# Clustered attention feeding a mixture of experts: expert scores as pairs of 64-row products, ten probability tiles, fixed banks and a new order

## The chip, the cores and the metric

The kernel runs on one core of one Trainium2 chip. A core has five engines that the text names: TensorE (PE; its weight loads are listed apart as PEld), VectorE (DVE), ScalarE (ACT), GpSimd (POOL) and SyncE (SP), which here only issues DMAs. The metric is device time in microseconds; the time of a kernel is the median of its runs.

## What is computed

```python
# clustered attention: batch 4, heads 8, sequence 768, head dim 64, 16 clusters per head
q_assign = argmax(einsum('bhsd,hcd->bhsc', normalized(q), normalized(centroids)))
k_assign = argmax(einsum('bhsd,hcd->bhsc', normalized(k), normalized(centroids)))
mask     = q_assign[:, :, :, None] == k_assign[:, :, None, :]
scores   = where(mask, q @ k.T / 8, -1e9)
attn_out = softmax(scores) @ v                         # per head
x        = attn_out as [batch, sequence, 512]
# mixture of experts: 4 experts of dim 64, causal attention in each, top 2 per token
logits = x @ w_gate
w      = softmax over the top 2 of logits
for e in range(4):
    qe, ke, ve = x @ wq[e], x @ wk[e], x @ wv[e]
    a   = softmax(where(causal, -1e9, qe @ ke.T / 8))
    out += (e is in the token's top 2) * w[e] * (a @ ve @ wo[e])
```

## The kernel before

The work is cut into 24 *pairs* n. The first 16 are pairs of attention heads (`attention_operands`), the last 8 pairs of experts (`moe_operands`), two to a batch; `core(n)` is common to both. The two heads (or experts) of a pair lie in rows 0 to 63 and 64 to 127 of the operand tiles.

*The order.* Every step is recorded as an operation of a `Plan`. A table of numbers, `ORDER`, then says in which order all operations are issued; each engine takes its own in that order, so an instruction that waits holds up all behind it on its engine. "~20" in the table stands for 20 fill matmuls (`spin`, L1150), which compute nothing that is used; "*" picks an operation's second engine. A second table, `SLOTS`, picks the buffer. PSUM has three double banks (`pp`, for scores, row scores and projections) and two single banks (`sg0`, `sg1`); which single bank a step gets is picked by `SLOTS`. The fills write sg0.

*An attention pair.* Per pair: k and q are turned by VectorE (L485, 128x768 with a strided writing side; pair 0 by TensorE, L494). The cluster of each row is found by a product with the centroids into a single bank (L520), which VectorE transposes into the other one (L524); a maximum, a comparison, a multiplication, a maximum and a one-hot comparison follow there (L531, L532, L533, L538, L539), then a transpose back (L527). ScalarE makes `rows` of it (L544), which go through DRAM (`rw`) into 16 rows of the operand tile `tk`. k and q themselves are each split into a rounded part (hi, ScalarE L333) and the rest (lo).

Row products (L887; two times two matmuls into one double bank: the hi parts, then 48 rows with the clusters) give a coarse score with queries on the partitions; VectorE takes its maxima (L900), gathers them (L906), turns them (L914), and a DMA puts them into a row of `tk`. The scores proper (L970) have keys on the partitions: per tile four steps (kh·ql, kh·qh, kl·qh, and 49 rows with clusters and maxima), each for both heads: the two matmuls of a step use rows 0 to 63 and 64 to 127 and run at the same time. ScalarE takes the exponential (L983) into a probability tile, GpSimd and VectorE add the tiles up (L338, L339), TensorE sums over keys (L1049, fp32, column tiles of 32) and multiplies with v (L1022, fp32, column tiles of 64; two recorded passes each). The results, normalised (L1099), go to DRAM as x, and from there to the expert part.

*An expert pair.* Projections of k and q for both experts together (L644, 12 full-height products into `pp` for each half of each), split by ScalarE and VectorE (L333, L653) into a staging tile `hl`. From there 10 DMAs a pair and two copies (L344, L345) put the parts of each expert one above the other, so that each of the two experts has full-height operands. The row products (L890, 80 rows) and the scores (L976: one step of 128 rows and one of 97) are full-height matmuls, one expert after the other. The causal triangle is added to the coarse scores by VectorE (L898). Their maxima are turned by TensorE (L928 into a single bank), negated by ScalarE or VectorE (L934, L937) and sent by DMA into a row of `tq`. GpSimd cuts the triangle out of the probabilities (L989). Values are projected at L694; the output product is L1137.

*Buffers.* Operand tiles `tk`, `tq` exist three times; attention uses them by n % 3, the experts two of them. Probability tiles are three of their own (p0 to p2) and, in turn, tiles lent by x (xh0 to xl2) or, for the experts, pieces of the third operand set.

## Time and profile before

| | before |
|---|---|
| median of three runs | 731.78 us (728.76, 731.78, 733.81) |
| profiled execution | 730.91 us, its span 729.2 us |
| TensorE busy | 683.1 us (94%) |
| VectorE busy | 496.7 us (68%) |
| GpSimd busy | 470.1 us (64%) |
| ScalarE busy | 294.4 us (40%) |
| mean granted TensorE clock | 0.979 |

The share of busy time is a mean over three stretches: the start up to about 55 us, the attention pairs to about 400 us, and the experts. Each has its own limit, so the rows below are taken by stretch. A busy TensorE is one that has matmuls in flight; what one of them costs is read from the distance of two starts.

### The profile page before, as it was taken

The page shows a single profiled execution, that of the slowest core. Times are in us where ns is not written, and L with a number is a line of the kernel's source. Part 1 is how long each engine was busy: PE and PEld are TensorE (multiplying, and loading weights), DVE is VectorE, ACT ScalarE, POOL GpSimd, SP SyncE. Part 2 cuts the span into 40 slices and gives each one's busy share as a digit, 9 for nine tenths or more (in the row PEclk, how much of TensorE's full clock was granted, in tenths as well). Part 3 has the DMA queues.
Part 4 walks back from the last instruction along what each step waited for, and adds up shares of the span by engine and source line. Part 5 has one row for each costly group of instructions (what it writes and reads, how often), then busy time and mean ns, then how long its engine had stood idle before and what let it go on. Part 6 is the DMA issues. An engine that isn't in the chain of part 4 may idle for free. (4 is left out here: it accounts for less than half of the span.)

```text
span 729.2 us, 13595 instructions
## 1 busy us (share of the span) xinstructions
PE 683.1 (94%) x5230; PEld 509.5 (70%) x5230; DVE 496.7 (68%) x808; ACT 294.4 (40%) x500; POOL 470.1 (64%) x344
## 2 busy tenths in 40 slices
PE   5589999999999999999999999989989799999997
PEld 4566667676767676766666777669668776797775
DVE  3577888697689889889787442554564376657843
ACT  2314464545554544454445153324141414242441
POOL 3227799999999987999995675761535433331420
PEclk9699999999999999999999999999899999999999
DMA  7134444165272445344142441433243435334423
GB/s 131 43 77 80 102 99 78 47 141 106 67 176 55 110 99 126 79 104 110 45 142 79 117 132 36 144 104 88 88 110 89 110 95 140 102 82 125 118 83 115
DMA packets 140729, 72.52 MB, mean 99 GB/s; under 512 B 116700, under 2 KB 125176, under 8 KB 140664
## 3 DMA queue, kind: packets, MB, share of 16 engines
q1 hardware_dynamic: 140664, 71.65, 39.4%
q8 instruction: 41, 0.67, 0.4%
q14 instruction: 24, 0.20, 0.1%
HBM read 39.68 MB, written 16.06 MB: 76 GB/s over the span
## 5 line engine op out<-in xcount | busy, mean ns | idle before, releaser
L900 DVE TENSOR_REDUCE mx<-pp 128x2 f32<-128x768 f32 (+1 forms) x224 | 206.0, 940 | 75.0 <-PE pp L887 65.6
L970 PE MATMUL pp<-tq,tk 64*128 64x384 f32 x1152 | 137.4, 343 | 1.4 <-DVE mx L900 0.7
L970 PEld LDWEIGHTS pp<-tq,tk 64*128 64x128 f32 x1152 | 98.9, 185 | 15.6 <-DVE mx L900 2.9
L983 ACT ACTIVATE p<-pp 128x768 f32<-128x768 f32 (+2 forms) x99 | 76.1, 787 | 73.5 <-PE pp L970 63.4
L887 PE MATMUL pp<-tk,tq 64*128 64x384 f32 x384 | 79.8, 412 | 2.6 <-DVE mx L900 1.8
L887 PEld LDWEIGHTS pp<-tk,tq 64*128 64x128 f32 x384 | 48.4, 248 | 38.6 <-issue 15.7
L983 ACT ACTIVATE xh<-pp 128x768 f32<-128x768 f32 x63 | 49.9, 814 | 61.2 <-PE pp L970 58.5
L338 POOL TENSOR_TENSOR acc<-acc,p 128x768 f32<-128x768 f32 (+1 forms) x36 | 62.9, 1747 | 13.4 <-DVE acc L339 7.5
L887 PE MATMUL pp<-tk 48*128 48x384 f32 x384 | 65.4, 337 | 0.0
L970 PE MATMUL pp<-tk 49*128 49x384 f32 x384 | 65.0, 335 | 0.0
L1022 PE MATMUL sg<-p,vt 128*64 128x384 f32 x308 | 56.2, 493 | 0.0
L976 PE MATMUL pp<-tq,tk 128*128 128x384 f32 (+5 forms) x288 | 51.6, 320 | 2.8 <-DVE M L900 1.2
L983 ACT ACTIVATE xl<-pp 128x768 f32<-128x768 f32 x45 | 35.5, 812 | 41.2 <-PE pp L970 35.8
L976 PEld LDWEIGHTS pp<-tq,tk 128*128 128x128 f32 (+1 forms) x288 | 45.4, 193 | 9.5 <-issue 3.2
L338 POOL TENSOR_TENSOR acc<-acc,xh 128x768 f32<-128x768 f32 x26 | 48.7, 1875 | 4.5 <-DVE acc L339 3.5
L887 PEld LDWEIGHTS pp<-tk 48*128 48x128 f32 x384 | 49.6, 255 | 0.0
L1022 PE MATMUL sg<-xh,vt 128*64 128x384 f32 x252 | 45.6, 490 | 0.0
L898 DVE TENSOR_TENSOR pp<-pp,tri 128x256 f32<-128x256 f32 x48 | 20.5, 427 | 32.5 <-PE pp L890 31.2
L1150 PE MATMUL sg<-onesb 128*128 128x128 bf16 x237 | 22.6, 270 | 16.6 <-DVE oh L539 11.1
L333 ACT ACTIVATE hl<-pp 128x384 fp32r<-128x384 f32 x18 | 8.9, 492 | 71.7 <-PE pp L644 46.4
L338 POOL TENSOR_TENSOR tk<-xk,tk 128x768 fp32r<-128x768 f32 (+1 forms) x14 | 24.7, 1765 | 20.0 <-ACT tk L333 20.0
L1022 PEld LDWEIGHTS sg<-p,vt 128*64 128x64 f32 x308 | 20.2, 136 | 24.7 <-issue 22.0
(259 smaller groups left out, 1564.3 us busy)
## 6 DMA issues: line engine op xcount, KB each, us to landing
tq<-hl SPq DMA_DIRECT2D x48, 192.0 KB
rb<-rd SPq DMA_DIRECT2D x46, 192.0 KB
vt<-in_v_dram SPq DMA_DIRECT2D x16, 384.0 KB
x<-xt SPq DMA_DIRECT2D x16, 384.0 KB
tk<-hl SPq DMA_DIRECT2D x32, 192.0 KB
kt<-in_k_dram SPq DMA_DIRECT2D x56, 96.0 KB
qt<-in_q_dram SPq DMA_DIRECT2D x56, 96.0 KB
out_dram<-xt SPq DMA_DIRECT2D x21, 256.0 KB
```

The lines of the kernel that those rows point to most:

```text
L333: return op("act", t_act(n, sbuf), lambda: ACT.activation(dst(), src(), AF.Copy), due, after, use, alt=(MO["m_copy"], "dve", t_dve(n), lam ...
L338: ways = [("pool", t_pool(n), lambda: POOL.tensor_tensor(dst(), a(), b(), op=fn)), ("dve", t_dve(n), lambda: DVE.tensor_tensor(dst(), a(), ...
L887: PE.matmul(ps()[:, h, :HW], at, kt[rs, i * HW:(i + 1) * HW], start=(j == 0), stop=(j == 1))
L898: DVE.tensor_tensor(e, e, tri[:, None, :].to_broadcast([128, 2, 128]), op=OP.add)
L900: DVE.tensor_reduce(to, ps()[:, :, :w], axis=AX.X, op=OP.max)
L970: PE.matmul(p()[:, h, :HW], kt[rs, kc * 128:(kc + 1) * 128], qt[rs, hf * HW:(hf + 1) * HW], start=(i == 0), stop=(i == 3))
L976: PE.matmul(p()[:, h, o_:HW], cols(K, rs, slot, h, kk, k0, k0 + 128), cols(Q, rs, slot, h, hf, o_, HW), start=(i == 0), stop=(i == 1))
L983: ACT.activation(pt()[:, :, o_:HW], p()[:, :, o_:HW], AF.Exp, scale=SC)
L1022: PE.matmul(av()[h * 64:(h + 1) * 64, o_:HW], d["vv"](h, kc), pt()[:, h, o_:HW], start=(kc == 0), stop=(kc == nk - 1), tile_position=(0, 6 ...
L1150: PE.matmul(single[0][:, HW:], onesb, onesb, start=True, stop=True)
```

## The change

1. *Expert operands.* The projections' hi and lo parts are written by ScalarE and VectorE straight into `tk` and `tq`, expert 0 in rows 0 to 63, expert 1 in rows 64 to 127, as attention has them. The staging tile, its DMAs and its copies go. Row products are two 64-row matmuls, one for each expert; scores are four steps of two matmuls, of 64 and at last 49 rows. Row products and scores may begin by halves (`need_row`, `need_st` have an entry for each half).
2. *Expert maxima.* They take attention's way: VectorE's transpose (L872) and a DMA into a row of `tk`.
3. *Operand sets* rotate by n % 3 throughout.
4. *Probability tiles.* Ten of their own, p0 to p9; the sums' tiles rotate over three. The AV products stand in one group of six tiles.
5. *Single banks.* sg0 (`brief`) has the AV results, the assignment, attention's sums and the fills; sg1 (`misc`) the transposed assignment, the experts' sums and the gate.
6. *Turns of x.* VectorE's transposes read and write 128x768 without a stride on the writing side; v is loaded by four DMAs of 32 partitions instead of one, and the normalised result is written in the matching order.
7. *Order.* New `ORDER` and `SLOTS`; 218 fills instead of 237.

Lines move: L520 is L517, L524 is L520, L539 is L535, L527 is L523, L485 is L478, L887 is L842, L890 is L846, L900 is L856, L914 is L872, L970 and L976 are L909, L983 is L915, L1022 is L953, L1049 is L980, L644 is L636, L694 is L676, L1150 is L1086.

```diff
+    def brief():
+        t = plan.buf(psum, "sa", (128, 512), FT, 1)
+        t.home = lambda: single[0]
+        return t
+
     def misc():
-        t = plan.buf(psum, "sg", (128, 512), FT, 2)
-        t.home = lambda: single[t.slot]
+        t = plan.buf(psum, "sb", (128, 512), FT, 1)
+        t.home = lambda: single[1]
         return t
...
     def set_of(n):
-        return n % 3 if n <= NA else (n - 1) % 2
+        return n % 3
...
                 def go(t=t, xx=xx):
-                    DVE.transpose(xx().rearrange("p (c j u) -> p c u j", c=NC, u=4),
-                                  t().rearrange("p (u c i) -> p c u i", u=4, c=NC))
+                    DVE.transpose(xx(), t().rearrange("p (u c i) -> p c u i", u=4, c=NC))
...
-        m1 = misc()
+            for u in range(4):
+                dma(d["v"]()[32 * u:32 * u + 32].rearrange("p h c d -> p h (c d)"),
+                    v[b, 2 * pr:2 * pr + 2].rearrange("h (j u c) d -> u j h (c d)", j=32, u=4)[u])
+        m1, m2, oh, sm = brief(), misc(), tmp("oh", (128, HW), BF), tmp("sm", (128, 2, G))
...
-                o = copy_op(lambda hf=hf: hi()[:, hf], lambda m=m, hf=hf: m()[:, hf, :HW], HW, due + 3 * hf + 1, [o], [m, hi])
+                hi, lo = [T[:, 0, i * S + hf * HW:i * S + (hf + 1) * HW] for i in range(2)]
+                o = copy_op(lambda hi=hi: hi, lambda m=m, hf=hf: m()[:, hf, :HW], HW, due + 3 * hf + 1, [o] + free, [m])
...
-        need_row = [put(K, low, 0, hi, t0 + MO["k"] + 5, his, [hi])]
-        need_st = [repeat(lambda h=h: K[low, 1, h], lambda h=h, hi=hi: hi()[h * D:(h + 1) * D].rearrange("p f j -> p (f j)"),
-                          S, t0 + MO["k"] + 6, his + free, hi) for h in range(2)]
-        need_st.append(put(K, high, 1, lo, t0 + MO["k"] + 6, los, [lo]))
+        kh, kl = project("k", K, t0 + MO["k"])
+        qh, ql = project("q", Q, t0 + MO["q"])
+        d["need_row"] = [kh[:1] + qh[:1], kh + qh[1:]]
+        d["need_st"] = [kh[:1] + kl[:1] + qh[:1] + ql[:1] + clear, kh + kl + qh[1:] + ql[1:] + clear]
...
     def p_tile(n):
-        own = ["p0", "p1", "p2"]
-        more = [] if n == 0 or n == NA - 2 else SPARE[:-1] if n < NA - 2 else [f"z{i}" for i in range(7)]
...
         ring[0] += 1
+        return wide(f"p{ring[0] % 10}")
...
                         for h in range(2):
-                            PE.matmul(ps()[:, h, :w], cols(Q, slice(0, D + NK), 0, h, hf, cc * 128, (cc + 1) * 128),
-                                      by_head(K)[0:D + NK, 0, h, i * w:(i + 1) * w], start=True, stop=True)
+                            rs = slice(h * D, (h + 1) * D)
+                            PE.matmul(ps()[:, h, :w], qh[rs, hf * HW + cc * 128:hf * HW + (cc + 1) * 128],
+                                      kh[rs, i * w:(i + 1) * w], start=True, stop=True)
...
-            def go(hf=hf, m=m):
-                PE.matmul(m()[:2 * HC, :128], M6[:, hf].rearrange("p h c -> p (h c)"), identr, start=True, stop=True)
+            def go(hf=hf, turned=turned):
+                if moe:
+                    DVE.transpose(turned(), M32[:, hf].bitcast(FT))
...
-                    for h in range(2):
-                        for i, (slot, nr) in enumerate(rows_of):
-                            rs = slice(0, nr)
-                            PE.matmul(p()[:, h, o_:HW], cols(K, rs, slot, h, kk, k0, k0 + 128), cols(Q, rs, slot, h, hf, o_, HW),
-                                      start=(i == 0), stop=(i == 1))
+                    for i, (nr, kt, qt) in enumerate(((D, kh, ql), (D, kh, qh), (D, kl, qh), (49, km, qm))):
+                        for h in range(2):
+                            rs = slice(h * D, h * D + nr)
+                            to, by = p()[:, h, o_:HW], qt[rs, hf * HW + o_:(hf + 1) * HW]
+                            if moe and i == 3:
+                                to = to.rearrange("p (c b j) -> p c b j", b=4, j=32)
+                                by = qt[rs, hf * HW:(hf + 1) * HW].rearrange("p (b c j) -> p c b j", b=4, j=32)[:, o_ // 128:]
+                            PE.matmul(to, kt[rs, kc * 128:(kc + 1) * 128], by, start=(i == 0), stop=(i == 3))
...
-                    av = misc()
+                    av = brief()
...
-            m = misc()
+            m = misc() if moe else brief()
```

*TensorE's start.* The row after a name's L number gives the instruction, the tile written, the tiles read, the size, and what it waits for. TensorE before, from the first pair's assignment (L520) to the first row product (L887); the runs of fills (L1150) are cut to their first:

```order
L520 MATMUL sg1_69<-xq_0_221,cbd_86 32x384 [waits Activation_49]
...
L1150 MATMUL sg0_68<-onesb_70 128x128 [waits DVE_49]
...
L520 MATMUL sg1_69<-xh2_0_250,cbd_86 32x384 x2
L520 MATMUL sg1_69<-xh3_0_264,cbd_86 32x384 x2
...
L520 MATMUL sg1_69<-xk_0_331,cbd_86 32x384 x2
L520 MATMUL sg1_69<-xq_0_344,cbd_86 32x384 x2
...
L887 MATMUL pp_2_436<-tk0_88,tq0_89 128x384 [waits Activation_49]
```

The same stretch of TensorE after (assignment L517, fills L1086, row product L842):

```order
L517 MATMUL sg0_68<-xk_0_224,cbd_85 32x384 [waits Activation_49,Pool_49]
...
L1086 MATMUL sg0_68<-onesb_70 128x128 [waits DVE_49]
...
L517 MATMUL sg0_68<-xh2_0_269,cbd_85 32x384 [waits DVE_49]
L517 MATMUL sg0_68<-xh2_0_269,cbd_85 32x384
L517 MATMUL sg0_68<-xh3_0_264,cbd_85 32x384 x2
...
L842 MATMUL pp_2_415<-tk0_87,tq0_88 128x384 [waits Activation_49]
```

Three assignments stood ahead of the first row product, with 52, 52 and 17 fills behind them, and wrote sg1; now two do, with 67 and 41 fills, and write the fills' bank sg0. The third pair's assignment now stands between the first row products.

*VectorE at the start.* Before, from the first pair's transposed assignment (L524) on; L485 are the turns of k and q of the next pairs:

```order
L524 STREAM_TRANSPOSE sg_68<-sg_69 128x384 [waits PE_49,Activation_49]
L485 STREAM_TRANSPOSE xh_0_250<-xh_0_183 128x6x4x32 [waits DMAHW3_49,DMAHW4_49,DMAHW2_49,DMAHW1_49]
L531 TENSOR_REDUCE sm_258<-sg_68 128x24 [waits DVE_49]
L532 TENSOR_TENSOR sg_68<-sg_68,sm_258 128x384 [waits DVE_49]
L533 TENSOR_TENSOR sg_68<-sg_68,ramp 128x384 [waits DVE_49,Pool_49]
L485 STREAM_TRANSPOSE xh_0_264<-xh_0_139 128x6x4x32 [waits DMAHW6_49,DMAHW7_49,DMAHW5_49,DMAHW0_49]
L538 TENSOR_REDUCE sm_258<-sg_68 128x24 [waits DVE_49]
L539 TENSOR_TENSOR oh_268<-sg_68,sm_258 128x384 [waits DVE_49]
L527 STREAM_TRANSPOSE ot_327<-oh_268 128x384 [waits DVE_49]
L485 STREAM_TRANSPOSE xk_331<-kt_225 128x6x4x32 [waits DMAHW5_49,DMAHW6_49,DMAHW0_49,DMAHW7_49,Activation_49,Pool_49]
```

VectorE after, from the same step on (L478 are the turns):

```order
L520 STREAM_TRANSPOSE sg_69<-sg_68 128x384 [waits PE_49,Activation_49]
L527 TENSOR_REDUCE sm_250<-sg_69 128x24 [waits DVE_49]
L528 TENSOR_TENSOR sg_69<-sg_69,sm_250 128x384 [waits DVE_49]
L529 TENSOR_TENSOR sg_69<-sg_69,ramp 128x384 [waits DVE_49,Pool_49]
L534 TENSOR_REDUCE sm_250<-sg_69 128x24 [waits DVE_49]
L535 TENSOR_TENSOR oh_260<-sg_69,sm_250 128x384 [waits DVE_49]
L523 STREAM_TRANSPOSE ot_262<-oh_260 128x384 [waits DVE_49]
L478 STREAM_TRANSPOSE xh_0_264<-xh_0_138 128x768 [waits DMAHW6_49,DMAHW7_49,DMAHW5_49,DMAHW0_49]
L478 STREAM_TRANSPOSE xh_0_269<-xh_0_227 128x768 [waits DMAHW6_49,DMAHW7_49,DMAHW5_49,DMAHW0_49]
L478 STREAM_TRANSPOSE xl_0_274<-xl_0_184 128x768 [waits DMAHW3_49,DMAHW4_49,DMAHW2_49,DMAHW1_49]
L478 STREAM_TRANSPOSE xl_0_351<-xl_0_254 128x768 [waits DMAHW3_49,DMAHW4_49,DMAHW2_49,DMAHW1_49]
L520 STREAM_TRANSPOSE sg_69<-sg_68 128x384 [waits PE_49]
```

The seven steps of the first pair now stand together; four turns instead of two and one stand behind them, ahead of the second pair's.

*TensorE among the experts.* Before, in the first pair of experts; tk1 and tq1 are the operands, L976 the scores, L1049 the sums, L1022 the AV products (vm the values):

```order
L976 MATMUL pp_0_5774<-tq1_91,tk1_90 128x128 [waits DVE_49]
L976 MATMUL pp_0_5774<-tq1_91,tk1_90 128x128 x3
...
L1049 MATMUL sg1_69<-acc0_0_5476,ones32_81 32x384 [waits Activation_49,Pool_49]
L1049 MATMUL sg1_69<-acc1_0_5662,ones32_81 32x384 [waits Pool_49]
...
L1022 MATMUL sg0_68<-p2_0_5757,vm_1_5238 64x384 [waits Activation_49,Pool_49]
```

The corresponding piece after; L909 are the scores, L846 the row products of the next pair (tk2, tq2), L980 the sums, L953 the AV products:

```order
L846 MATMUL pp_1_5802<-tk2_91,tq2_92 128x384 [waits Activation_49]
L846 MATMUL pp_1_5802<-tk2_91,tq2_92 128x384
L980 MATMUL sg0_68<-acc0_0_5434,ones32_81 32x384
...
L846 MATMUL pp_2_5815<-tk2_91,tq2_92 128x512 [waits Activation_49]
L846 MATMUL pp_2_5815<-tk2_91,tq2_92 128x512
L909 MATMUL pp_0_5820<-tq1_90,tk1_89 128x128 [waits DVE_49]
L909 MATMUL pp_0_5820<-tq1_90,tk1_89 128x128 x5
L909 MATMUL pp_0_5820<-tk1_89 128x128 x2
L953 MATMUL sg0_68<-p2_0_5777,vm_0_5335 64x384 [waits Activation_49,Pool_49]
```

A tile of scores was four full-height matmuls and is eight of half height; row products of the next pair stand among them, and the last attention pair's sums (L980) and the next AV group (L953) now follow each other in sg0, where they had sg1 and sg0.

## Rows read from the trace of the kernel before

**Rows 1.** Windows: us; busy us of each engine (instructions); granted clock, DMA share, GB/s
```profile
0.00:55.00 55.00, 36.41 (x345) 30.07 (x347) 29.48 (x56) 13.26 (x22) 16.80 (x23) 0.88 0.44 84
55.00:400.00 345.00, 342.12 (x2948) 234.11 (x2943) 284.54 (x390) 173.70 (x255) 312.20 (x189) 1.00 0.42 98
400.00:500.00 100.00, 92.81 (x661) 75.12 (x658) 47.36 (x79) 32.20 (x65) 66.46 (x50) 1.00 0.35 97
500.00:600.00 100.00, 90.91 (x550) 74.66 (x549) 53.85 (x110) 28.45 (x66) 39.92 (x43) 0.93 0.39 105
600.00:729.20 129.20, 120.87 (x739) 95.50 (x737) 81.49 (x177) 46.77 (x95) 34.67 (x41) 0.99 0.38 108
```
**Rows 2.** Waits of PE, 0 to 55 us: line, releaser; us in total, times, longest
```profile
PE sg L1150 <- DVE oh L539: 11.1, 2, 6.2
```
**Rows 3.** Timeline of PE, 11 to 43: start, us, instruction, count, [idle before]
```profile
20.86 5.51 PE L1150 MATMUL sg<-onesb 128*128 128x128 bf16 x52 [6.21 <-DVE oh L539]
26.30 0.85 PE L520 MATMUL sg<-xh,cbd 128*32 128x384 f32 x8
32.02 5.07 PE L1150 MATMUL sg<-onesb 128*128 128x128 bf16 x52 [4.88 <-DVE oh L539]
...
40.38 1.11 PE L1150 MATMUL sg<-onesb 128*128 128x128 bf16 x17 [2.51 <-DVE sg L533]
41.42 0.51 PE L887 MATMUL pp<-tk,tq 64*128 64x384 f32 x2
```
**Rows 4.** Timeline of DVE and of SP's queue, 14 to 28
```profile
14.77 0.60 DVE L524 STREAM_TRANSPOSE sg<-sg 128x384 f32<-128x384 f32 x1 [9.93 <-PE sg L520]
15.28 1.52 DVE L485 STREAM_TRANSPOSE xh<-xh 128x768 f32<-128x768 f32 x1
...
20.84 0.58 DVE L527 STREAM_TRANSPOSE ot<-oh 128x384 bf16<-128x384 bf16 x1
...
24.58 0.80 SPq L316 DMA_DIRECT2D tk<-rw  x2
```
**Rows 5.** Timeline of PE, 429 to 437: pairs of attention scores, then two changes of mode
```profile
429.72 0.69 PE L970 MATMUL pp<-tq,tk 64*128 64x384 f32 x6
...
430.43 0.69 PE L970 MATMUL pp<-tq,tk 64*128 64x384 f32 x6
...
433.41 0.33 PE L887 MATMUL pp<-tk 48*128 48x384 f32 x2
433.67 0.85 PE L1049 MATMUL sg<-acc,ones 128*32 128x384 f32 x8
434.45 0.39 PE L694 MATMUL pp<-wvh,xh 128*128 128x260 f32 x1
434.68 0.28 PE L694 MATMUL pp<-wvh,xl 128*128 128x260 f32 x1
434.80 0.28 PE L694 MATMUL pp<-wvl,xh 128*128 128x260 f32 x1
```
**Rows 6.** The line L890: count, ns min/median/max, first and last start, forms
```profile
L890 PE MATMUL pp<-tk,tq x128: 223/337/659, 442.8 to 685.7; 80*128 80x384 f32 x48, 80*128 80x320 f32 x32, 80*128 80x512 f32 x16, 80*128 80x256 f32 x16
```
**Rows 7.** The page's costliest groups: busy us, mean ns of one, idle before
```profile
L900 DVE TENSOR_REDUCE mx<-pp 128x2 f32<-128x768 f32 (+1 forms) x224 | 206.0, 940 | 75.0 <-PE pp L887 65.6
L970 PEld LDWEIGHTS pp<-tq,tk 64*128 64x128 f32 x1152 | 98.9, 185 | 15.6 <-DVE mx L900 2.9
L983 ACT ACTIVATE p<-pp 128x768 f32<-128x768 f32 (+2 forms) x99 | 76.1, 787 | 73.5 <-PE pp L970 63.4
```
**Rows 8.** Groups by line and shape, 150 to 350 us: the copies of AV results
```profile
L333 ACT ACTIVATE avu<-sg 128x384 f32<-128x384 f32 x12 | 5.9, 494 | 5.8 <-PE sg L1022 5.8
```
**Rows 9.** Waits of PE, 400 to 729.2: us in total, times, longest
```profile
PE sg L928 <- ACT avu L333: 4.3, 1, 4.3
PE pp L890 <- DVE mx L900: 2.2, 2, 1.7
PE pp L890 <- DVE hl L653: 1.3, 1, 1.3
```

More of the change, by code (lines that the diff above doesn't have):

```diff
@@ L802, in last_half @@
         d["a"].append(o)
-    ring, part = [0], {}
-    def piece(i):
-        name = "tk2" if i < 4 else "tq2"
-        if name not in part:
-            part[name] = sb.tile([128, 4, 2, HW], FT, name=name, bufs=1)
-        return part[name][:, i % 4]
-    def wide(tag):
-        t = tmp(tag, (128, 2, HW) if tag[0] != "x" else (128, S), FT if tag[0] != "x" else FR)
-        if tag[0] == "x":
-            t.view = lambda a: a[:, :].bitcast(FT).rearrange("p (h c) -> p h c", h=2)
-        elif tag[0] == "z":
-            t.home = lambda: piece(int(tag[1:]))
-        return t
-    def p_tile(n):
-        own = ["p0", "p1", "p2"]
-        more = [] if n == 0 or n == NA - 2 else SPARE[:-1] if n < NA - 2 else [f"z{i}" for i in range(7)]
-        if part.get("more") != more:
-            part["more"], ring[0] = more, 0
-        i = ring[0] % (len(own) + len(more))
+    ring = [-1]
+    def wide(tag):
+        return tmp(tag, (128, 2, HW))
+    def p_tile(n):
         ring[0] += 1
-        t = wide((own + more)[i])
-        if n == NA - 1 and t.home is not None:
-            part.setdefault("first", {}).setdefault(t.args[1], t)
-        return t
+        return wide(f"p{ring[0] % 10}")
     def acc_tile(n, hf):
-        third = SPARE[-1] if n < NA - 2 else "z7"
-        if n == 0 or n == NA - 2:
-            return wide(("acc0", "acc1")[hf])
-        return wide(("acc0", "acc1", third)[(2 * n + hf) % 3])
+        return wide(f"acc{(2 * n + hf) % 3}")
     def ends(n, hf):
```

361 lines of the change are left out of this document (155 added, 206 removed), and 4 rows, old and new, of the table ORDER.

## The prediction

> **What bounds the kernel now.** I read the windows first, then the waits of TensorE, then timelines of the stretches where it does wait. The windows [rows 1] cut the span at its three regimes. From 55 to 400 us, the sixteen attention pairs, TensorE is busy 342.1 of 345.0 us at full granted clock; GpSimd with 312.2 comes next. Nothing but work taken off TensorE can shorten that stretch. From 0 to 55 us it is busy 36.4, so 18.6 us are start-up. From 400 to the end it is busy 92.8 + 90.9 + 120.9 = 304.6 of 329.2, which leaves 24.6 us of waits, and the clock was 0.93 in the middle hundred. The change can gain at three places: the start, the expert pairs' TensorE work, the expert stretch's waits.
>
> At the start the waits [rows 2] name one cause: the fill matmuls wait 11.1 us, two times, for VectorE's one-hot product L539. The timeline shows why that is on the path: 52 fills stand at 20.86 after an idle 6.21, 52 more at 32.02 after 4.88, and the first row product comes at 41.42 [rows 3]. What that product needs was there long before: the pair's cluster rows were issued to its operand by 24.58 + 0.80 = 25.4 [rows 4]. The fills do no work for the result, but TensorE takes them in order, so the product stands behind them and behind the second pair's assignment.
>
> **The change, part by part.**
>
> *Start.* Before, the assignment writes sg1, and the fills, on sg0, wait for the bank that VectorE turns the assignment into, until L539 has read it. After, the assignment itself writes sg0, so the fills behind it wait only for VectorE's first transpose, which ends at 14.77 + 0.60 = 15.4 [rows 4]. A fill there takes 5.51/52 = 0.106 us [rows 3]: 67 of them end at 22.5. The second pair's assignment (0.85 us in its own row before) ends near 23.4. VectorE meanwhile does the first pair's seven steps in one go: the two shown took 0.60 and 0.58 [rows 4], so with their small gaps they end near 19.5 rather than at 20.84 + 0.58 = 21.4. Two turns of x follow before that assignment can begin. Each took 1.52 in the strided form [rows 4]; the unstrided one is bounded below by the 0.60 of a half-size plain transpose. Even two at 1.52 end at 22.6, so the assignment is not delayed by more than 0.1. Two more turns stand ahead of the second transpose; it therefore ends between 24.2 and 25.7 (23.4 plus a hand-over and 0.60, or 22.6 + 3.0 + 0.1). The last 41 fills take 41 x 0.106 = 4.4 at that pace, or 41 x 1.11/17 = 2.7 at that of the row at 40.38. The first row product starts between 26.9 and 30.1; I take 28.8, later than the middle since the turns are likelier nearer 1 us than 0.6. That is 12.6 earlier than 41.4. The third pair's assignment now lies inside the row products, and three-fold more issues of v stand in SP's queue ahead of the maxima: I take off 0.6. **-12 us**, between -8 (the maxima's DMAs late by a load burst of a few us) and -14.5. Whatever comes after is bound by TensorE, so the shift stays; rival A is that it does not.
>
> *Row products of the experts.* Before, 128 products of 80 rows, two heads one after the other: 48 of 384 columns, 32 of 320, 16 each of 512, 256 and 128 [rows 6], 43,008 columns. A full-height product advances 260 columns in 434.80 - 434.68 = 0.12 us [rows 5], 0.46 ns a column: 19.8 us. After, the two heads use 64 rows each and run together: eight 64-row products of 384 columns, four pairs, take 430.43 - 429.72 = 0.71 [rows 5], 0.178 a pair, the price of one full-height product. So half goes: **-9.8**. The end of nothing gained: if what is paced is not TensorE but VectorE's reduces (0.940 for 768 columns [rows 7], against 0.18 for the pair) the gain is 0.
>
> *Scores of the experts.* 288 full-height products become 288 concurrent pairs: four steps a tile before and after, 0. The narrow tiles (256 and 128 columns, 128 of the pairs) are not seen as pairs: if no pair goes below 0.178 they cost up to 128 x 0.06 = 7.5 more; if they go with their columns, 0. The fourth pair now reads its moving side strided, which no row shows: 0 to +5 (72 such pairs at up to 0.07). The pair's loads overlap (below), so I take the lower ends: **+1**.
>
> *Maxima of the experts.* The sixteen transposes L928 on TensorE go: 16 x 128 columns x 0.46 ns = **-1.0**. VectorE transposes the maxima instead, 128x192, work it already does for attention; it has idle time there (its busy time is 182.7 of 329.2 after 400 [rows 1]). If that cover is gone it costs at most the 0.60 of the larger transpose in [rows 4] each time, sixteen times.
>
> *Switches of height.* Going between 64-row pairs, full height and column tiles costs time: the last row pair at 433.41 is followed by L1049 0.26 later rather than 0.18, and the first L694 at 434.45 has 0.23 to the next, rather than 0.12 [rows 5]. 0.08 + 0.11 = 0.19. Along TensorE's order I count 192 such changes before and 223 after; the expert scores now stand between full-height projections. 31 x 0.19 = **+5.9** (+3 to +9: which pair of modes is switched varies). The Trainium skill, page "TensorEngine Tiling (Array Packing)", section Tiling Modes, states that changing the mode drains the engine; the trace agrees, with 0.08 us for the drain. By the page's text alone, which gives no price, the term would stay open.
>
> *Fixed banks.* AV sums, assignment and attention's sums now share sg0. Between an AV group and the next use of its bank stand ScalarE's copy, 0.494 [rows 8], and its hand-over. In the order some twenty such turns leave TensorE only about 1 us of other work, the rest (some 60) several us. If the copy stands behind one exponential of 0.787 [rows 7], 0.49 + 0.79 passes 1 by 0.3: at one time in three, twenty turns give **+2**; 0 to +8.
>
> *Waits of the expert stretch.* Its largest wait, L928 for an AV copy, 4.3 us [rows 9], falls with its instruction; the rows' waits for `hl` (1.3) and maxima (2.2) [rows 9] change form: no DMA lies between a projection and its row product any more (80 issues go), rows begin when their own half is there. The ten probability tiles relieve waits on exponentials, which are small. I take **-5** of 24.6, between -12 and 0.
>
> *Attention's steady state.* The products are the same. The turns of x get shorter on VectorE, which isn't the bound: 0.
>
> Sum against the profiled execution (span 729.2 and 1.7 around it, 730.9): 730.9 - 12 - 9.8 + 1 - 1.0 + 5.9 + 2 - 5 = 712.0. The median shown is 0.9 above that execution, so **713**.
>
> **Rivals.**
> *A. The start's gain is given back.* The first pairs would then wait for GpSimd or for loads. For it: GpSimd is busy 90% of 55 to 400 [rows 1]. Against: it is still less than TensorE, and also starts earlier. If 11 of the 12 return: 724.
> *B. The rows gain nothing*, since VectorE paces them: each 768-column tile is reduced in 0.940 [rows 7] while a pair is made in 0.18. Against: other products stand between the row products. 713 + 9.8 = 723. With narrow pairs at the full price, 729.
> *C. Slower: the turns of sg0.* Some 80 groups go through the one bank. The gain left, 19 us, and the 1% make 26: at (19 + 7)/80 = 0.33 us lost on each turn the kernel is slower by over 1%. One copy behind one exponential does that only where the next user comes within 1 us; it would need all 80 to be so, or copies that wait two exponentials. 740.
> *D. The pairs' weight loads are not hidden.* A 64x128 load takes 0.185 us [rows 7]. If each of the 352 new pairs (64 row, 288 score) showed it, +65: 778. Against: in [rows 5] four pairs with eight such loads take 0.71 in all, so the loads lie under other products of the same rows. The Trainium skill, page "TensorE: Matmul & The Clock Gate", section Part 3 on packing small matmuls, says that a load overlaps running products only where its row group differs, which would speak for D. The trace of attention's scores contradicts it, with 0.178 a pair.
>
> **How the numbers follow.** The forecast 0.55 (its own range 703 to 721, from the ends of start, waits, switches and narrow pairs, which seldom fall on one side together); better still, with waits at -12 and the start at -14.5, 0.05 (about 701); A 0.13; B 0.15; C 0.08; D and the like 0.02; what remains, 0.02, no change. A measurement tells about 1% (7 us) from no change: faster means under 724.5. A and B lie on that line, and I give half of each to either side: faster 0.55 + 0.05 + 0.14 = 0.74; same 0.14 + 0.02 = 0.16; slower 0.08 + 0.02 = 0.10. The range 702 to 728 leaves out the better case, C, D and the tail of B, some 0.18.
>
> **What would show it.** Right: the first row product near 29 us, with the fills' waits of 11.1 gone; attention's stretch as long as before; TensorE's busy time lower by some 5 to 10 after the attention pairs; L928's wait gone. Wrong: waits on the AV copy at L953 or L517 summing over 5 us (C), waits on the reduce L856 ahead of L846 of several us (B), a first expert score later than 12 us ahead of before's (A), or 64-row score pairs of 384 columns stepping by over 0.25 (D).

## The result, and the profile after

The changed kernel takes 682.25 us (median of four runs, 680.71 to 683.31) beside 732.79 for the kernel before on the same chip: a ratio of 0.931, with a 95% interval of 0.925 to 0.937. It was forecast at 713, with a range of 702 to 728. The direction was right, the size was not: 50 us instead of 19.

Two lines of its page, its span and TensorE's busy time:

```profile
span 679.0 us, 13938 instructions
PE 660.0 (97%) x5483; PEld 490.2 (72%) x5483; DVE 472.9 (70%) x800; ACT 301.0 (44%) x503; POOL 455.8 (67%) x331
```

Its windows, cut where its own regimes change (stretch, us; busy us of PE, PEld, DVE, ACT, POOL; granted clock, DMA share, GB/s):

```profile
0.00:42.50 42.50, 35.25 (x362) 28.49 (x364) 29.52 (x59) 16.31 (x26) 16.29 (x22) 1.00 0.76 125
42.50:376.00 333.50, 332.82 (x2890) 230.45 (x2890) 264.78 (x385) 174.78 (x253) 306.22 (x184) 1.00 0.43 99
376.00:679.00 303.00, 291.92 (x2237) 231.22 (x2229) 178.57 (x359) 109.88 (x225) 133.33 (x126) 1.00 0.19 61
```

These answer to [rows 1]. TensorE's busy time fell by 23 us and the span by 50, so most of what went was time in which TensorE did nothing, or worked slowly. In the attention pairs TensorE had 2.9 us without work and now has 0.7. In the expert stretch it had 24.6 and now has 11.1, and the granted clock, which was 0.93 in the middle hundred, is 1.00 everywhere. This execution is the fastest of the four; two others had granted clocks of 0.997 and 0.995 over the whole span and took some 2.5 us longer. TensorE's busy time behind the attention pairs fell by 12.7 us, where the prediction's sign was 5 to 10.

TensorE's timeline at the start (start, us, instruction, count, idle before it), answering to [rows 3]:

```profile
15.25 3.90 PE L1086 MATMUL sg<-onesb 128*128 128x128 bf16 x67 [0.79 <-DVE sg L520]
20.63 0.85 PE L517 MATMUL sg<-xh,cbd 128*32 128x384 f32 x8 [1.48 <-DVE xh L478]
22.83 2.45 PE L1086 MATMUL sg<-onesb 128*128 128x128 bf16 x41 [1.34 <-DVE sg L520]
25.21 0.51 PE L842 MATMUL pp<-tk,tq 64*128 64x384 f32 x2
...
35.38 0.44 PE L909 MATMUL pp<-tq,tk 64*128 64x384 f32 x2
```

The 67 fills begin at 15.25, as forecast, and the first row product comes at 25.2, 3.6 us earlier than forecast and 16.2 earlier than before. What holds it up now are VectorE's turns (1.48) and transposes (1.34). The 67 fills take 3.90/67 = 0.058 us each.

TensorE's waits of the changed kernel behind its start (engine, line, releaser; us, times, longest):

```profile
PE pp L846 <- ACT vm L683: 1.8, 2, 0.9
PE sg L723 <- DVE wt L719: 1.5, 1, 1.5
PE pp L636 <- DVE mx L856: 1.2, 2, 0.6
PE pp L909 <- ACT xt L335: 0.9, 3, 0.4
PE pp L909 <- DVE tq L645: 0.8, 1, 0.8
```

Nothing of [rows 9] is left but small pieces: L928's 4.3 fell with its instruction, and no product is listed as waiting for a copy of AV results; the weight loads of the AV groups (L953) stood 0.9 us for one, four times in all. Waits on maxima are 1.2.

### The profile page after: what moved, and what is told of

Read it like the earlier page. It is cut to its first block, busy times and chain, and to the rows that moved or that the text cites. A ratio compares the mean times of both kernels' runs of the same rounds, so it can differ in the third digit from the quotient of the medians.

```text
span 679.0 us, 13938 instructions
## 1 busy us (share of the span) xinstructions
PE 660.0 (97%) x5483; PEld 490.2 (72%) x5483; DVE 472.9 (70%) x800; ACT 301.0 (44%) x503; POOL 455.8 (67%) x331
## 4 chain that ended last, share of the span: by engine, by line
PE 92%; DVE 3%; ACT 2%; DMA 1%; issue 1%; SPq 0%; DVEq 0%; ACTq 0%
PE pp L909 26%; PE sg L953 24%; PE pp L842 13%; PE pp L636 10%; PE pp L1073 5%; PE pp L676 5%; PE sg L980 3%; PE pp L846 2%; PE sg L517 2%; PE sg L1086 2%; DMA tk<-rw 1%; DVE mx L856 1%; ACT p L915 1%; DMA rd<-r 0%; PE pp L486 0%
## 5 line engine op out<-in xcount | busy, mean ns | idle before, releaser
L856 DVE TENSOR_REDUCE mx<-pp 128x2 f32<-128x768 f32 (+1 forms) x224 | 207.4, 941 | 83.5 <-PE pp L842 73.6
L340 POOL TENSOR_TENSOR acc<-acc,p 128x768 f32<-128x768 f32 (+2 forms) x136 | 235.5, 1737 | 30.4 <-DVE acc L341 23.8
L915 ACT ACTIVATE p<-pp 128x768 f32<-128x768 f32 (+2 forms) x264 | 190.5, 774 | 139.5 <-PE pp L909 138.2
L909 PE MATMUL pp<-tq,tk 64*128 64x384 f32 (+2 forms) x1584 | 183.2, 336 | 2.4 <-ACT xt L335 0.9
L909 PEld LDWEIGHTS pp<-tq,tk 64*128 64x128 f32 x1584 | 133.4, 185 | 20.8 <-ACT p L915 7.4
L953 PE MATMUL sg<-p,vt 128*64 128x384 f32 x768 | 130.9, 490 | 0.0
L340 POOL TENSOR_TENSOR acc<-p,p 128x768 f32<-128x768 f32 (+1 forms) x42 | 75.9, 1807 | 41.7 <-ACT p L915 38.7
L953 PEld LDWEIGHTS sg<-p,vt 128*64 128x64 f32 x768 | 52.3, 137 | 63.4 <-issue 61.0
L909 PE MATMUL pp<-tk 49*128 49x384 f32 (+2 forms) x528 | 88.0, 328 | 0.0
L842 PE MATMUL pp<-tk,tq 64*128 64x384 f32 x384 | 78.3, 402 | 0.0
L842 PEld LDWEIGHTS pp<-tk,tq 64*128 64x128 f32 x384 | 48.7, 248 | 34.6 <-issue 14.6
L842 PE MATMUL pp<-tk 48*128 48x384 f32 x384 | 66.2, 338 | 0.4 <-DMA tk<-rw 0.4
L842 PEld LDWEIGHTS pp<-tk 48*128 48x128 f32 x384 | 50.1, 254 | 0.8 <-DMA tk<-rw 0.7
L909 PEld LDWEIGHTS pp<-tk 49*128 49x128 f32 x528 | 50.2, 185 | 0.0
L953 PE MATMUL sg<-p,vm 128*64 128x384 f32 (+2 forms) x288 | 39.7, 420 | 0.1
L953 PEld LDWEIGHTS sg<-p,vm 128*64 128x64 f32 x288 | 19.3, 136 | 19.1 <-issue 15.1
L676 PE MATMUL pp<-wvh,xh 128*128 128x260 f32 x96 | 27.3, 284 | 0.0
```

The costliest lines, as they stand in the source:

```text
L340: ways = [("pool", t_pool(n), lambda: POOL.tensor_tensor(dst(), a(), b(), op=fn)), ("dve", t_dve(n), lambda: DVE.tensor_tensor(dst(), a(), ...
L676: PE.matmul(m()[:, c % 2, :NV], x_[dc]()[:, ts], w_[:, dc, :], start=(i == 0), stop=(i == 3 * DC - 1))
L842: PE.matmul(ps()[:, h, :HW], at, kt[rs, i * HW:(i + 1) * HW], start=(j == 0), stop=(j == 1))
L856: DVE.tensor_reduce(to, ps()[:, :, :w], axis=AX.X, op=OP.max)
L909: PE.matmul(to, kt[rs, kc * 128:(kc + 1) * 128], by, start=(i == 0), stop=(i == 3))
L915: ACT.activation(pt()[:, :, o_:HW], p()[:, :, o_:HW], AF.Exp, scale=SC)
```

## The experiments

All times are medians of four runs. They come from four sessions, in which the kernel before had 731.0 to 733.0, so differences of under 1.5 us between sessions mean little. "Longer than the changed kernel" always compares with its 682.25 of the section on the result. Where a trace is quoted, the shift inside it (how much later the same instruction starts than in the trace of the changed kernel) is the better number. Lines that an edit shifts have other numbers in such a trace; the operation and the tiles identify them.

**1. The banks of the first three assignments alone, in the kernel before.** Six digits of `SLOTS` are turned, so that the assignment m1 goes to sg0 and its transpose m2 to sg1 for the first three pairs:

```diff
 SLOTS = """
-0101011010110101101010110101001101000111110001101011001001100011001010001101100110000111010001110000101111101110110111
+0011010110101101101010110101001101000111110001101011001001100011001010001101100110000111010001110000101111101110110111
```

> The kernel before, with the first three pairs' assignments written to sg0 (the fills' bank) and their transposes to sg1, nothing else changed. Theory (the start is bound by fills that wait for the one-hot product in their bank): the fills then wait only for the first transpose, the first row product comes at about 32 us instead of 41.4, and the whole is 9 to 13 us shorter, 718 to 722. Rival (a gain at the start is given back by later waits): the first row product is earlier but the whole time is within 3 us of before.

722.06 us, ratio 0.988 (0.983 to 0.993) to before, so 9.4 shorter. TensorE's timeline:

```profile
15.61 3.06 PE L1150 MATMUL sg<-onesb 128*128 128x128 bf16 x52 [0.78 <-DVE sg L524]
...
23.64 4.57 PE L1150 MATMUL sg<-onesb 128*128 128x128 bf16 x52 [2.62 <-DVE sg L524]
...
30.75 0.51 PE L887 MATMUL pp<-tk,tq 64*128 64x384 f32 x2
```

The fills wait for the first transpose (L524), no longer for the one-hot product, and the first row product comes 10.7 earlier. At the last sums the shift is still 9.0, so what the start gains is not given back.

**2. The fills in sg1, in the changed kernel.**

```diff
-        PE.matmul(single[0][:, HW:], onesb, onesb, start=True, stop=True)
+        PE.matmul(single[1][:, HW:], onesb, onesb, start=True, stop=True)
```

> The changed kernel, with its fills in sg1, the bank in which VectorE works on the assignment, so that they wait for the one-hot product again. Theory (wait and clock): the 67 fills start near 19.5 instead of 15.3 and run at half clock after the long wait (0.106 us each), the first row product comes near 35 instead of 25.2, the whole is 9 to 11 us longer than the changed kernel. Rival (the wait alone counts, the clock stays): fills at 0.058, first row product near 30, 5 us longer.

685.49 us, 3.2 longer than the changed kernel. TensorE's timeline:

```profile
16.31 5.53 PE L1086 MATMUL sg<-onesb 128*128 128x128 bf16 x67 [3.83 <-DVE oh L535]
...
26.31 3.80 PE L1086 MATMUL sg<-onesb 128*128 128x128 bf16 x41 [3.69 <-DVE oh L535]
30.04 0.67 PE L842 MATMUL pp<-tk,tq 64*128 64x384 f32 x2
```

The waits on the one-hot product are back and the fills run slower (5.53 for 67 instead of 3.90), but the first row product is only 4.8 later, and the shift settles at 3.9 by the later sums. The theory's numbers were too high, and the rival's 30 and 5 were nearer, though the fills did run slower. VectorE has the seven steps in one go in the new order, so its one-hot product comes 5 us behind the start of the assignment, not 6; this assignment also lay 2.3 us earlier in this execution. The bank is worth 9 us in the old order and 3 to 4 in the new one. Even with the bank's wait the first row product comes 11.4 earlier than before (9.1 without that earlier assignment), so the new order carries a large part of the gain by itself: VectorE's seven steps in one go, plain turns, and one assignment and 13 fills fewer ahead of that product. Of these only the turns were tried alone (experiment 4).

**3. Every row product of the experts twice.**

```diff
-                        for h in range(2):
+                        for h in (0, 1, 0, 1):
```

> The changed kernel, with every row product of the experts issued twice (the second pair repeats the first one's result): 128 more 64-row matmuls, 21,500 columns of pairs. Theory (TensorE bounds the expert stretch and pairs are priced by columns): 9.9 us longer than the changed kernel. Rival (VectorE's reduces pace these tiles): less than 3 us longer.

688.95 us, 6.7 longer; the span grows by 7.8. The line in its trace:

```profile
L846 PE MATMUL pp<-tk,tq x256: 215/333/502, 410.9 to 645.2; 64*128 64x384 f32 x48, 64*128 64x320 f32 x32, 64*128 64x512 f32 x16, 64*128 64x256 f32 x16
```

Sixty-four more pairs cost 0.10 to 0.12 us each, a fifth to a third less than their columns say. The window of the expert stretch shows why (engines as in the windows above):

```profile
376.00:686.80 310.80, 301.12 (x2365) 240.62 (x2357) 178.03 (x359) 109.19 (x225) 132.85 (x126) 1.00 0.19 59
```

TensorE's busy time rises from 291.9 to 301.1, by 9.2, which is near the 9.9; its time without work falls from 11.1 to 9.7, as some of the added pairs stand where it waited before. So TensorE bounds the stretch, the pairs cost about their columns, and VectorE's reduces don't pace these tiles (rival B falls).

**4. Strided turns again, in the changed kernel.**

```diff
-                    DVE.transpose(xx(), t().rearrange("p (u c i) -> p c u i", u=4, c=NC))
+                    DVE.transpose(xx().rearrange("p (c j u) -> p c u j", c=NC, u=4),
+                                  t().rearrange("p (u c i) -> p c u i", u=4, c=NC))
```

> The changed kernel, with the turns of k and q strided again, as before (1.58 instead of 0.95 us each on VectorE), v loaded by one DMA and the results written in the old order. Theory (only the start has no cover for them): two turns stand ahead of the second pair's assignment and two ahead of its transpose, so the first row product is 1 to 2 us later and the whole 1 to 2 us longer than the changed kernel; attention's stretch stays. Rival (the shorter turns and spread loads matter all along): 4 us or more.

689.97 us, 7.7 longer: four times what I expected. TensorE's timeline at its start:

```profile
22.45 0.85 PE L518 MATMUL sg<-xh,cbd 128*32 128x384 f32 x8 [2.58 <-DVE xh L478]
25.75 4.53 PE L1087 MATMUL sg<-onesb 128*128 128x128 bf16 x41 [2.45 <-DVE sg L521]
30.21 0.69 PE L843 MATMUL pp<-tk,tq 64*128 64x384 f32 x2
```

With four turns of 1.6 instead of 0.95 the first row product comes at 30.2, 5.0 later. About 2 of these are the 41 fills at 4.53 instead of 2.45, behind waits that add up to 5 us; 0.7 was there before any of these turns (the 67 fills begin at 15.96 and not at 15.25). At the first sums the shift is 6.5, and it grows to 7.7 through attention: there the turns matter little, as I had said. At the start I had expected 1 to 2 us, and they are worth some 6. The edit's other two parts, v's single load and the old order of the results, were not tried apart from the turns.

**5. Thirty-seven changes to full height and back**, each one fill between two 64-row products of the expert stretch, in unused columns of sg1. A new step of the order, "!1", stands at 37 places:

```diff
+    def extra(step):
+        def full(other):
+            PE.matmul(single[1][:, HW:], onesb, other, start=True, stop=True)
+        if step[0] == "!":
+            for _ in range(int(step[1:])):
+                full(onesb)
+            return
...
```

> The changed kernel, with 37 single fill matmuls (128 rows, 128 columns, into the unused columns of sg1) put between neighbouring 64-row products of the expert stretch, so that each adds a change to full height and one back. Theory of the prediction (a change of height costs 0.19): 37 x (0.06 + 2 x 0.19) = 16 us longer than the changed kernel. Rival (these changes cost next to nothing, which is why the 33 more of the expert stretch don't show in its time): 37 x 0.06 = 2 us longer.

692.24 us, 10.0 longer; the span grows by 11.5.

```profile
L1104 PE MATMUL sg<-onesb x37: 229/230/230, 423.0 to 653.3; 128*128 128x128 bf16 x37
```

So (10.0 to 11.5)/37 = 0.27 to 0.31 for a fill of 0.06 and two changes: 0.11 to 0.13 a change between these two heights. It isn't free, and it isn't 0.19. I had added the readings of two different changes: 0.08 from 64-row pairs to column tiles, and 0.11 from column tiles to full height.

**6 and 7. A made wait near 513 us, idle and filled.** The same chain twice over: matmul, ScalarE's copy of 128 columns, a DMA, a matmul that reads it.

Here `full` is one matmul into sg1; `rounds` is 2 in both kernels, and `fills` is 0 in the first and 45 in the second.

```diff
...
+        rounds, fills = [int(c) for c in step[1:].split("/")]
+        full(onesb)
+        other = onesb
+        for r in range(rounds):
+            ACT.activation(w_a, single[1][:, HW:], AF.Copy)
+            SP.dma_start(w_b, w_a)
+            for _ in range(fills):
+                PE.matmul(single[1][:, HW:], onesb, onesb, start=True, stop=True)
+            full(w_b)
```

> The changed kernel, with a made wait near 513 us, ahead of a run of 12 values, 24 projections and 60 values, all full height: twice in a row TensorE writes 128 columns of sg1, ScalarE copies them, a DMA moves the copy, and a matmul needs it; that leaves TensorE idle some 5 us. Theory (a wait of several us is paid twice, as half clock stands behind it): projections behind it step 0.22 to 0.35 instead of 0.175 for some us, the granted clock of the 10 us behind it is below 0.9, and the whole is 7 to 9 us longer. Rival (a wait costs itself): clock 1.0, 5 us longer or less.

> The same made wait as in the run before it, with 45 fill matmuls put into each of its two halves, so that TensorE isn't idle while the copy and the DMA run. Theory (a wait is paid twice because of the idle engine): clock 1.0 behind it, the whole 5 to 6 us longer than the changed kernel and 2 to 4 us shorter than the run with the idle wait. Rival (the clock has nothing to do with it): both runs are equally long within 1 us.

689.05 us idle, 687.59 filled: 6.8 and 5.3 longer than the changed kernel. The idle one's timeline, and then two of its windows:

```profile
515.24 0.23 PE L1102 MATMUL sg<-w_b,onesb 128*128 128x128 bf16 x1 [2.15 <-DMA w_b<-w_a]
517.58 0.29 PE L1102 MATMUL sg<-w_b,onesb 128*128 128x128 bf16 x1 [2.11 <-DMA w_b<-w_a]
...
518.20 0.42 PE L684 MATMUL pp<-wvl,xh 128*128 128x260 f32 x1
518.41 0.42 PE L684 MATMUL pp<-wvh,xh 128*128 128x260 f32 x1
...
521.33 0.52 PE L644 MATMUL pp<-xh,wkh 128*128 128x384 f32 x1
521.65 0.52 PE L644 MATMUL pp<-xl,wkh 128*128 128x384 f32 x1
```

```profile
515.00:520.00 5.00, 2.65 (x13) 2.53 (x14) 1.87 (x6) 0.66 (x2) 0.00 (x0) 0.55 0.05 8
520.00:525.00 5.00, 5.00 (x25) 5.00 (x25) 0.00 (x0) 0.00 (x0) 0.75 (x1) 0.77 0.56 160
```

The filled one's timeline and window:

```profile
514.25 2.67 PE L1114 MATMUL sg<-onesb 128*128 128x128 bf16 x45 [0.36 <-ACT w_a L1111]
...
520.25 0.28 PE L684 MATMUL pp<-wvl,xh 128*128 128x260 f32 x1
520.37 0.28 PE L684 MATMUL pp<-wvh,xh 128*128 128x260 f32 x1
```

```profile
515.00:520.00 5.00, 4.58 (x83) 4.46 (x80) 2.60 (x7) 0.66 (x2) 0.00 (x0) 1.00 0.07 14
```

The idle wait is two pieces without work of 2.15 and 2.11 us, one small matmul between them, 4.7 us in all. Behind it the values step 0.21 and the projections 0.32, half the pace of 0.12 and 0.175, until 522.2; the clock of these windows is 0.55 and 0.77, so much of them is at the lower of the two levels, 1.2 instead of 2.4 GHz. After the filled wait, which is longer (513.65 to 519.92, 6.3 us), they step 0.12 and the clock is 1.00. The half clock costs 11 x 0.1 + 6 x 0.145 = 2.0 us on top of a wait of 4.7: the wait is paid nearly one and a half times, not twice. As the filled chain is itself 1.6 longer, the two should differ by only 0.4, and I had expected 2 to 4: across the made wait the shift grows by 6.2 in the idle trace and by 5.6 in the filled one. The totals can't settle so little; their ranges overlap (686.9 to 690.3, 687.1 to 688.0), and the idle kernel's trace has half clock once more, far behind the edit:

```profile
665.00:675.00 10.00, 10.00 (x75) 8.14 (x76) 4.69 (x12) 1.85 (x3) 0.00 (x0) 0.83 0.26 92
```

TensorE is without a wait there. So an idle wait is one thing that half clock stands behind, and not the only one.

**8. A stage between projection and operand**, through SP's queue, with the rests computed behind the DMA.

```diff
...
+                ACT.activation(mid(), src(), AF.Copy)
...
+            dma(dst[:D], mid()[:D])
+            dma(dst[D:], mid()[D:])
```

> The changed kernel, with the rounded parts of the experts' projections staged again: written to a tile of their own and moved into the operands by two DMAs for each half (64 more issues), with the rest computed from the operand after it. Theory (the expert stretch's waits fell because no DMA lies between a projection and its row product): 13 us of waits and half clock come back in part, 6 to 10 us longer than the changed kernel, with waits of row products and scores on those DMAs. Rival (the new order has enough work between a projection and its use to hide 2 to 3 us, so the waits fell by the order): less than 2 us longer.

760.91 us, 79 longer: far outside what either expected.

**9. The same stage, with its DMAs in ScalarE's queue and the rests taken from the stage.**

```diff
...
+            ACT.dma_start(dst[:D].bitcast(FT), mid()[:D].bitcast(FT))
+            ACT.dma_start(dst[D:].bitcast(FT), mid()[D:].bitcast(FT))
```

> The changed kernel, with the rounded parts of the experts' projections staged in one tile and moved into the operands by two DMAs for each half, this time issued from ScalarE's own queue, so that SP's queue holds nothing else up; the rests are computed from the stage, not after the DMA. In a few places the second half's copy has overwritten the stage by then, so those rests are taken from the wrong half (the same work on other numbers). Theory (the waits fell because no DMA lies between a projection and its row product): 6 to 10 us longer than the changed kernel, in waits of row products and of copies on these DMAs and the half clock behind them. Rival (the order hides 2 to 3 us, and the run before was slow by SP's queue and by rests that waited for the DMA): less than 3 us longer.

720.58 us, 38 longer. ScalarE's waits in this run show what went wrong with it as a test:

```profile
ACT hl L341 <- DMA tk<-hl: 17.4, 5, 9.5
ACT hl L341 <- DMA tq<-hl: 14.5, 3, 8.9
```

There was room for one stage only, so a copy waits until the DMAs of the one before have read it, 32 us in all, and all that stands behind it on ScalarE waits too. In experiment 8 the same copies wait 21.5 us for these DMAs and 24.6 more for the rests. Neither run says what a DMA's delay alone costs.

**10. Without the 67 and the 41 fills.**

```diff
-0 6 110 5 4 112 ~20 1 3 ~3 10 11 12 208 2 15 16 ~24 7 8 9 111 ~13 22 23 24 209 25 26 114 27 13 113 29 17* 210 115 ~67
-120 207 14 211 30 121 31 18* 213 122 21 20* 304 117* 123 ~41 42 40 124 36 19* 43 125 116 37 126 ~9 38 305 212 217 39
+0 6 110 5 4 112 ~20 1 3 ~3 10 11 12 208 2 15 16 ~24 7 8 9 111 ~13 22 23 24 209 25 26 114 27 13 113 29 17* 210 115
+120 207 14 211 30 121 31 18* 213 122 21 20* 304 117* 123 42 40 124 36 19* 43 125 116 37 126 ~9 38 305 212 217 39
```

> The changed kernel without the 67 and the 41 fills ahead of the first row product. Theory (an idle engine is followed by half clock, and the first row product waits for the cluster rows' DMA near 25 us anyway): TensorE idles from 15 to 20 and from 21 to 25, the clock of 20 to 45 us falls below 0.95, and the whole is 2 to 4 us longer. Rival (the fills only hold the queue): the same time within 1 us, or shorter.

684.15 us, 1.9 longer (682.66 to 688.0, so the ranges overlap). The window of 20 to 40 us:

```profile
20.00:40.00 20.00, 17.75 (x136) 11.70 (x138) 18.23 (x26) 7.63 (x11) 10.62 (x9) 0.73 0.56 116
```

The clock there falls to 0.73, as expected, but it costs little: the shift is 1.7 from 29 us on and 0.8 from 135 us on. The first row products wait 1.4 for the cluster rows' DMA, until 24.4, so the fills did little more than hold time that is waited out anyway. The 108 fills are worth a microsecond or two of the start's gain, and the rest isn't theirs.

**11 and 12. A small DMA's delay**, on the way from a projection to its row product: 128 x 4 numbers of the rounded part are written once more by a DMA, from ScalarE's queue and from SP's.

```diff
...
+                ACT.activation(s, src()[:, :4], AF.Copy)
...
+            ACT.dma_start(dst[:, :4].bitcast(FT), s.bitcast(FT))
```

> The changed kernel, with a DMA's delay alone between a projection and its row product: the rounded part is still written straight into the operand, but its first four columns are written once more by a DMA of 128 x 4 numbers from ScalarE's queue, so that row products and scores wait for one DMA (some 2 us, as the made wait of the earlier run showed) after the copy. No stage is shared, the rests don't wait, and the two extra steps for each half take 0.2 us and an issue of 0.5 on ScalarE. Theory (the waits fell because no DMA lies there): 6 to 10 us longer than the changed kernel. Rival (the order has other work for these 2 us; the two staged runs were slow by their one shared stage): less than 3 us longer.

> The same delay, with the 32 small DMAs issued from SP, behind whose head all other DMAs stand while it waits for the copy. Theory (DMA latency is what counts): as the run before it within 2 us. Rival (SP's order counts, as in the kernel before, which had 80 such issues in that queue): at least 4 us longer than the run before it.

690.19 and 688.76 us: 7.9 and 6.5 longer; at the last sums of their traces the shifts are 6.2 and 6.6. TensorE's waits in the first of them, from 370 us on:

```profile
PE pp L866 <- ACT vm L703: 3.1, 3, 1.6
PE sg L743 <- DVE wt L739: 2.1, 2, 1.9
PE pp L866 <- ACT p L935: 1.5, 1, 1.5
PE pp L929 <- DVE tq L665: 1.4, 2, 1.2
```

The small DMA, which no product waits for by name, brings back 6 to 8 us. Behind 376 us TensorE's time without work goes from 11.1 to 15.5 and 14.6, and the granted clock from 1.00 to 0.99 and 0.98. It makes no difference beyond the noise which queue holds the DMA, so it isn't SP's order. The waits are not put down to the DMA but to copies and exponentials that come late. The edit also gives ScalarE and VectorE a small extra step for each half; a kernel with those steps and without the DMA was not run, so the delay is not told apart from them.

## Why the prediction was wrong, step by step

Three terms failed: the pace of the fills at the start (-12 forecast, -16.4 measured), the waits of TensorE (-5, measured -15.7), and half clock in the expert stretch, which had no term (some -8).

**The start: forecast -12, measured -16.4** (first scores at 51.7 and 35.4). The mechanism was right: fills that wait for the one-hot product in their own bank. Experiment 1 gives 9.4 for it alone, in the old order. What was mis-sized is the pace of the fills. The forecast gave each of the 67 fills 0.106 us, from a row behind an idle 6.21, and had them end at 22.5. They took 0.058 and ended near 19.2, and the last 41 took 2.45 instead of 2.7 to 4.4. The windows show why, first before, then after:

```profile
20.00:25.00 5.00, 4.14 (x40) 4.14 (x40) 2.81 (x4) 1.44 (x2) 0.26 (x1) 0.50 0.12 43
15.00:20.00 5.00, 3.90 (x67) 3.72 (x66) 4.72 (x9) 1.11 (x2) 0.00 (x0) 1.00 0.53 65
```

The row of 0.106 stands at half clock (0.50), and the changed kernel's fills, behind a wait of 0.79, at 1.00. With the fills done early the turns of x came onto the path, which the forecast had ruled out: the assignment waited 1.48 for one. That is where the strided turns of experiment 4 cost some 6 us. The single runs can't be added up to 16.4, as the bank alone is worth 9.4 in the old order and 3 to 4 in the new. The gain was not given back (rival A falls): the shift is 16.4 at the first scores and 19.5 after four fifths of attention's, and the first expert score comes at 441.1 instead of 464.8. The stretch is bound by TensorE as before.

**Row products of the experts: forecast -9.8, about right.** Experiment 3 adds 9.2 us of busy time for 64 such pairs. The distances from each start at this line to TensorE's next start, less its idle time, add up to 25.5 before and 17.4 after: -8.1, changes of height and half clock included.

**Narrow and strided pairs: forecast +1, measured 0.** From TensorE's timeline after, each step's fourth pair (49 rows) being the strided one:

```profile
475.84 0.69 PE L909 MATMUL pp<-tq,tk 64*128 64x384 f32 x6
476.37 0.34 PE L909 MATMUL pp<-tk 49*128 49x384 f32 x2
476.55 0.52 PE L909 MATMUL pp<-tq,tk 64*128 64x256 f32 x6
476.91 0.28 PE L909 MATMUL pp<-tk 49*128 49x256 f32 x2
477.02 0.41 PE L909 MATMUL pp<-tq,tk 64*128 64x384 f32 x2
```

In the median over the trace, two starts of score pairs of 128, 256 and 384 columns lie 0.112, 0.119 and 0.175 us apart, and those of full-height products in the trace before 0.112, 0.121 and 0.177; the strided fourth pairs step 0.111, 0.118 and 0.178. Rival D (weight loads not hidden) falls with the same numbers. The rule of the Trainium skill that would have spoken for it ("TensorE: Matmul & The Clock Gate", Part 3) holds for none of these pairs.

**Switches: forecast +5.9.** The step that failed is the sum of 0.08 and 0.11: these were read at two different changes. By experiment 5 a change between 64-row pairs and full height costs 0.11 to 0.13. The Trainium skill ("TensorEngine Tiling (Array Packing)", Tiling Modes) says that a change of mode drains the engine; this run shows that it costs something. The 31 more changes are of three kinds, counted along the two traces: between 64 rows and full height 24 before and 49 after, between 64 rows and column tiles 118 and 159, between full height and column tiles 50 and 15. Only the first kind has a measured price, 25 x 0.12 = 3.0 us; what the other two gave or took is not shown.

**Fixed banks: forecast +2, measured 0.9 at most.** That is what the AV groups' weight loads wait for a copy; no product is listed with such a wait. Rival C, whose sign was 5 us, falls.

**Waits of the expert stretch: forecast -5. This is the step that failed most.** TensorE's time without work falls by 24.6 - 11.1 = 13.5 in the expert stretch, and by 2.2 in attention. And the sum had no term at all for the clock. In the trace before, L928's wait of 4.3 us is followed by values at half pace (timeline of the kernel before):

```profile
571.77 0.23 PE L928 MATMUL sg<-identr,M 128*6 128x128 f32 x1 [4.31 <-ACT avu L333]
...
572.73 0.42 PE L694 MATMUL pp<-wvl,xh 128*128 128x260 f32 x1
572.95 0.42 PE L694 MATMUL pp<-wvh,xh 128*128 128x260 f32 x1
```

The values step 0.22 there and 0.12 elsewhere [rows 5]. I had read the clock of 0.93 and 0.99 in [rows 1] and left it at that. Taken as a share of two levels, 0.93 over 100 us means 14 us at half clock and 0.99 over 129 us another 2.6: with TensorE busy, an estimate of 8 us of work lost. In the profiled execution all of it is gone, as the clock after is 1.00. Experiments 6 and 7 show that an idle wait can bring it: 4.3 us without work within 4.7 were followed by half clock until 4.6 us behind them, a filled wait of 6.3 by none. It isn't the whole cause. The half clock of 0.99 stands behind no wait in the kernel before, but behind a row of products of one column each (the last of its longer groups in the timeline, then the window):

```profile
710.65 0.81 PE L778 MATMUL pp<-ones,tq 128*128 128x1 f32 x6
710.00:715.00 5.00, 5.00 (x37) 3.83 (x37) 3.94 (x10) 0.00 (x0) 0.00 (x0) 0.71 0.29 108
```

The 0.93 is made up of three falls, at 517, 545 and 572 us, that do stand behind waits, of 0.9 us, of 1.1 and 1.0 close together, and of 4.3.

Together, against the profiled execution: start -4.4 beside the forecast, waits -10.7, clock -8.3, row products +1.7. That is -21.7, and the forecast's 712.0 and the profiled 680.7 differ by 31.3. The other 9.6 are a remainder and not a measurement: the terms that I had against the change (narrow pairs, switches, banks, +8.9 in the forecast) would have to come to about -0.7 in all. As the switches between 64 rows and full height alone should be +3.0, some 4 us were gained that I can't name.

What made the waits fall is shown in part. L928's 4.3 fell with its instruction. A DMA's delay between projection and row product, with the two small steps around it, is worth 6 to 8 us in the new order (experiments 11 and 12), waits and half clock together, so the direct operands are likely a large part of it. What the third operand set and the new order give by themselves was not isolated: an order is written for its buffers, and an old buffer scheme can't be put under the new order without changing what is computed. Of the 22 us of waits and half clock that the expert stretch lost, some 10 stay unassigned between these two.

## What to carry to other kernels

Read the granted clock beside every duration that you carry over to another kernel: a fill at 0.106 us was one at half clock, and 0.058 was its pace where it was needed. Price a wait of TensorE at what stands behind it too: read the granted clock in the windows that hold the wait and those behind it, and look whether steps there are longer. When a table of orders is rewritten along with the buffers, the waits that the old trace shows are no bound on what the new order can remove; take the whole idle time of the stretch as the far end, not the waits that one can name. Work that paces the first useful product counts in full, since nothing runs beside it (strided turns, some 6 us); fills that stand where the product would wait anyway count for next to nothing (experiment 10).

## What the runs showed of the hardware

- Behind two pieces without work of 2.15 and 2.11 us, one small matmul between them, TensorE ran at half pace for 4.6 us (clock 0.55 and 0.77 in these windows); behind 6.3 us in which fills ran, at full pace.
- Half clock also stood behind a row of one-column products without a wait (clock 0.71 from 710 to 715 us in the kernel before).
- VectorE's 128x768 transpose took 0.95 us with a plain written side and 1.58 with a strided one.
- A change between 64-row and full-height products cost 0.11 to 0.13 us in the changed kernel.
- Pairs of 64-row products step with their columns like one full-height product (0.112, 0.119 and 0.175 us for 128, 256 and 384 columns), and the strided moving side of the last pair costs nothing more.
